# Attention and gated MLP on one core: one planner for all pairs of heads, and score products of 128 rows

## The chip, the core and the metric

The kernel runs on one core of one Trainium2 chip. TensorE (PE) does the matrix products; its weight loads (PEld) run beside them. VectorE (DVE) and ScalarE (ACT) do the element-wise work, GpSimd (POOL) a few constants, and SyncE (SP) issues the transfers. Each engine works through its own list of instructions in order and waits at semaphores for the others. The metric is the device time of one execution in microseconds (us); lower is better.

## The reference

```python
# q, k, v: (4 batches, 8 heads, 768 tokens, 64), n_sink = 4, window = 128
scores = (1 / np.sqrt(D)) * np.matmul(q, k.transpose(0, 1, 3, 2))
keep = is_sink | in_window               # first 4 keys, or 0 <= i - j < 128
scores = np.where(keep, scores, -1e9)
a = exp(scores - max);  a = a / (sum(a) + 1e-09)
attn = np.matmul(a, v)                   # then laid out as x: 3072 tokens x 512
h = x @ w_in                             # 512 x 2048
g = h * np.clip(h + 3.0, 0.0, 6.0) / 6.0
out = g @ w_out                          # 2048 x 512
```

All of it is float32.

## The kernel before, in words

**Tiles.** A *unit* is 256 tokens of one batch: 12 units. The first tokens of the four batches come first (units 0 to 3), then the other eight. A *pair* is two heads of one unit: 48 pairs, four to a unit. A pair goes through these steps, named by the letters of the task table: `kq` and `v` load K, Q and V; `C` makes the scores on PE (line 497, tile `sp`); `t` masks and finds the minimum (DVE, L507), `m` merges the two windows (L515), `x` is the exponential (ACT, L524), `c` the reciprocal sums, `n` scales the rows (L538/L540); `D` transposes the probabilities on PE (L562, tile `pt`); for pairs of later units `p` multiplies by a side mask (L572, tile `pm`); `o` and `ol` split the result into a high and a low part (L195, L598, tiles `ph` and `pl`); `E` multiplies by V on PE (L640, tile `av`); `a`, `b`, `y`, `xh`, `xl` add up and split the result into the MLP's input `xh` and `xl`. A unit's MLP has 8 chunks; in each, `F` is 2 halves of 12 products (L698, tile `hps`), then `r`, `s`, `h`, `g` on ACT and DVE (L707 to L716), and `G` is 2 halves of 6 products (L730, tile `o`).

**Precision.** Values are split into a high and a low float32r part, and a product is the sum of three partial products. Pairs 0 to 11 use plain float32 products for attention instead. The scores of pairs 12 to 47 are three partial products for each of two heads and two tiles of queries. K and Q of the two heads lie on partitions 0 to 63 and 64 to 127, so each of these products uses 64 rows of the array:

```python
terms = [(d["qt"][:, i, ts], d["kt"][:, j, ks]) for i, j in ((0, 0), (1, 0), (0, 1))]
for j, (l, r) in enumerate(terms):
    for g in range(2):
        gs = slice(D * g, D * (g + 1))
        nc.tensor.matmul(out=sp[g][:, 0:w], lhsT=l[gs], rhs=r[gs], ...)
```

**Order.** Two mechanisms set the order. For pairs 0 to 13, the 32 parts of the weights and the MLP of units 0 and 1, `first_tasks` lists tasks with a cost, what they come after, a due number and what room they take (PSUM banks, buffers). `in_order` goes through time: whenever an engine is free it takes the ready task with the lowest due number that has room. Until planned time 30 (`QUIET`) an idle PE gets a filler product (tile `idle`, L245). A weight part is loaded (`w`), rebuilt from 64-bit words on ACT and DVE (`wa` to `wd`, L333 to L341) and split (`wh`, `wl`, L346). From pair 14 on `STAGES` writes the order by hand: eight stages for a pair, in which three pairs overlap (prepare, score, multiply by V), and `drain(1)` puts one half of an MLP chunk behind each stage. So each pair brings two chunks of MLP.

The names `wih`/`wil` and `woh`/`wol` are the high and low parts of the 8 chunks of both weights, `kt` and `qt` the split K and Q, `kr` and `qr` what was loaded.

Of the kernel before, what the change touches and what calls it, by code (L numbers as in the profile page):

```python
# [28 lines left out]
PAIRS = 14  # L29
NF32 = 12  # L30
PART_DUE = (5.4, 14.1, 33.8, 61.6, 65.3, 70.3, 72.6, 72.7, 75.9, 78, 80, 86.7, 102.5, 103.4, 105.5, 115, 115.2, 116.3,
            118.3, 119.3, 120.2, 122.7, 123.4, 124.1, 124.2, 124.4, 141.9, 161.5, 187.6, 205, 220.3, 236.5)
LEAD = {"kq": 39.1, "v": 38.1, "w": 38.8}
QUIET = 30.0
ROOM = {"kq": 2, "V": 2, "vr": 1, "split": 1, "bank": 7, "pl": 2, "Pt": 1, "ph": 2, "st": 3, "vs": 1, "wt": 3, "gf": 2,
        "gh": 2, "x0": 2, "x1": 2, "x2": 2, "x3": 2}


def first_tasks():
# [7 lines left out]
    for s in range(PAIRS):  # L47
        d = 10 * s
        f32 = s < NF32
        add(f"kq{s}", "SP", 0.95, [], d - LEAD["kq"], ("kq",))  # L50
        add(f"v{s}", "SP", 0.47, [], d - LEAD["v"], ("V",) if f32 else ("V", "vr"))
        start = [f"kq{s}"]
        if not f32:
            add(f"kh{s}", "ACT", 0.31, [f"kq{s}"], d - 1, ("split",))
            add(f"kl{s}", "DVE", 0.335, [f"kh{s}"], d - 1)
            add(f"qh{s}", "ACT", 0.31, [f"kq{s}", f"kh{s}"], d - 1)
            add(f"ql{s}", "DVE", 0.335, [f"qh{s}"], d - 1, (), ("kq",))
            add(f"vh{s}", "ACT", 0.31, [f"v{s}"], d + 3)
            add(f"vl{s}", "DVE", 0.335, [f"vh{s}"], d + 3, (), ("vr",))
            start = [f"kl{s}", f"ql{s}"]  # L60
        if s == PAIRS - 1:
            continue
        hold = ("pl", "pl") if f32 and s % 2 else ("Pt",)
        add(f"C{s}", "PE", 0.8 if f32 else 1.0, start, d, ("bank",) * 4 + hold, ("kq",) if f32 else ("split",), 0.35)
        for t in range(2):
            for h in range(2):
                add(f"t{s}.{t}{h}", "DVE", 0.345 if t else 0.21, [f"C{s}", "mask"], d + 0.1, (), ("bank",))
                add(f"x{s}.{t}{h}", "ACT", 0.49 if t else 0.385, [f"t{s}.{t}{h}"], d + 0.2)
        add(f"c{s}", "DVE", 0.41, [f"x{s}.{t}{h}" for t in range(2) for h in range(2)], d + 0.3, lag=0.1)
        for h in range(2):  # L70
            for t in range(2):
                add(f"n{s}.{t}{h}", "*", (0.41, 0.27) if t else (0.3, 0.2), [f"c{s}"], d + 0.4 + 0.01 * h)
            gives = hold[h:h + 1] if len(hold) == 2 else hold if h else ()
            add(f"D{s}.{h}", "PE", 0.4, [f"n{s}.0{h}", f"n{s}.1{h}"] + [f"D{s}.0"] * h, d + 0.5,
                ("bank", "ph") if f32 else ("bank", "ph", "pl"), gives)
            if f32:
                add(f"o{s}.{h}", "ACT", 0.37, [f"D{s}.{h}"], d + 0.6, (), ("bank",))
            else:
                add(f"o{s}.{h}", "ACT", 0.41, [f"D{s}.{h}"], d + 0.6)
                add(f"ol{s}.{h}", "DVE", 0.45, [f"o{s}.{h}"], d + 0.6, (), ("bank",))  # L80
        if f32:
            add(f"E{s}.0", "PE", 0.68, [f"o{s}.0", f"v{s}"], d + 0.7, ("bank", f"x{s % 4}"), ("ph",))
            add(f"E{s}.1", "PE", 0.68, [f"o{s}.1", f"E{s}.0"], d + 0.7, (), ("ph", "V"))
            add(f"xh{s}", "ACT", 0.27, [f"E{s}.1"], d + 0.8)
            add(f"xl{s}", "DVE", 0.334, [f"xh{s}"], d + 0.9, (), ("bank",))
    for k in range(32):
# [9 lines left out]
    for n in range(2):  # L96
        xs = [f"xl{4 * n + p}" for p in range(4)]
        for i in range(8):
            d = 1000 + 100 * n + 5 * i
            before = [f"F{n}.{i - 1}.1"] if i else []  # L100
            add(f"F{n}.{i}.0", "PE", 1.42, xs + before + [f"wl{4 * i}", f"wl{4 * i + 1}"], d, ("bank",))
            add(f"F{n}.{i}.1", "PE", 1.42, [f"F{n}.{i}.0"], d + 0.1, (), ("x0", "x1", "x2", "x3") if i == 7 else (), 0.25)
            add(f"r{n}.{i}", "ACT", 0.57, [f"F{n}.{i}.1"], -50, ("gf",))
# [3 lines left out]
            before = [f"G{n}.{i - 1}.1"] if i else []  # L107
            add(f"G{n}.{i}.0", "PE", 1.4, before + [f"g{n}.{i}", f"wl{4 * i + 2}", f"wl{4 * i + 3}"], d + 1.5,
                () if i else ("bank", "bank"))
            add(f"G{n}.{i}.1", "PE", 1.4, [f"G{n}.{i}.0"], d + 1.6, (), ("gh",))  # L110
        for t in range(2):
            add(f"O{n}.{t}", "ACT", 0.54, [f"G{n}.7.{t}"], -50, ("st",), ("bank",))
# [4 lines left out]
def in_order(tasks):  # L117
# [15 lines left out]
    while marks:  # L133
# [9 lines left out]
        while moved:  # L143
            moved = False
            for k, e in enumerate(engines):
# [25 lines left out]
                if gives:  # L171
                    heapq.heappush(freed, (end, count, gives))
                    heapq.heappush(marks, end)
# [31 lines left out]
def attn_ffn_kernel(ctx: ExitStack, tc: tile.TileContext, qx, kx, vx, vfx, vsx, n_sink, window, w_in, w_out, out):  # L205
# [190 lines left out]
    XHF = "A"  # L396
# [4 lines left out]
    def A_kq(s):  # L401
# [5 lines left out]
        st_[s].update(kr=kr, qr=qr)  # L407

# [15 lines left out]
    def A_split(s, part=None):  # L424
        if "vr" not in st_[s]:
            return
        hi, lo, src = st_[s]["vr"]
        if part != 1:
            copy_r(nc, nc.scalar, hi, src)
        if part != 0:  # L430
            nc.vector.tensor_tensor(out=lo, in0=src, in1=hi.bitcast(F32), op=ALU.subtract)
            del st_[s]["vr"]

    def B_k(s, part=None):
        if plain(s):
            return
        w = ncol(pus[s][1])
        d = st_[s]  # L440
# [32 lines left out]
    def C_score(s):  # L473
# [3 lines left out]
        d["nb"], d["sm"], d["rc"] = (work.tile([P, 4], F32, name=x, bufs=3) for x in ("nb", "sm", "rc"))  # L477
        if not plain(s):
            d["P"] = work.tile([P, 2, 2, WP], F32, name="Pt", bufs=1)
        elif s % 2:  # L480
            d["P0"], d["P1"] = (work.tile([P, 3 * P], F32, tag="pl", name="Ph") for h in range(2))
        else:
            both = work.tile([P, 2, 3 * P], F32, tag="Pt", name="Ph", bufs=1)
            d["P0"], d["P1"] = both[:, 0, :], both[:, 1, :]
        d["sp"] = []
        for t, (k0c, w, m) in enumerate(spans(u)):
# [569 lines left out]
```

## Time and profile before

| | us |
|---|---|
| median of 3 runs | 707.57 (707.29 to 707.86) |
| the profiled execution's own time | 706.91 |
| its span, first to last instruction | 705.1 |
| PE busy | 695.7 (99%) |
| PE weight loads busy | 618.5 (88%) |
| DVE busy | 514.7 (73%) |
| ACT busy | 455.8 (65%) |

The span is what the instructions cover; the execution's own time has some 1.8 us around it. Matmuls are pipelined: one lasts longer than the distance to the next, so busy PE time says little, and the distance from start to start is what counts. Granted TensorE clock was 0.998 of full speed over the span.

### The profile page before, as it was taken

To read this page: it belongs to the slowest core of one execution; us is meant where nothing else is said; L and a number is where in the kernel's file an instruction comes from. 1 tells how busy PE (TensorE), PEld (TensorE's weight loads), DVE (VectorE), ACT (ScalarE), POOL (GpSimd) and SP (SyncE) were. 2 spreads that over 40 slices of the span, in tenths; PEclk is the share of its full clock that TensorE was granted. 3 is DMA by queue.
4 is the path that set the end of the run, shared out by engine and by line. 5 is a ranking of instruction groups with operands and counts; after the bars stand their busy time and mean duration, and the time that the engine had idled before them with its cause. 6 is when DMAs were issued, how large, how long until landed. Compare 5 with 4: busy or idle time off the path is not lost.

```text
span 705.1 us, 13207 instructions
## 1 busy us (share of the span) xinstructions
PE 695.7 (99%) x4908; PEld 618.5 (88%) x4908; DVE 514.7 (73%) x1359; ACT 455.8 (65%) x1203; POOL 4.5 (1%) x18
## 2 busy tenths in 40 slices
PE   8999999999999999999999999999999999999996
PEld 7888988889898889898989898989898989899995
DVE  5999997455678778777877788778777877785221
ACT  5999886665576666657666667567656765764222
POOL 2000000000000000000000000000000000000000
PEclk9999999999999999999999999999999999999999
DMA  7665562220111101211111112111110111100000
GB/s 253 196 215 190 192 202 70 76 68 27 43 61 61 32 31 61 63 41 62 32 59 64 31 43 76 46 32 61 56 48 31 61 54 39 61 13 2 31 1 34
DMA packets 29608, 49.69 MB, mean 70 GB/s; under 512 B 3552, under 2 KB 20448, under 8 KB 29536
## 3 DMA queue, kind: packets, MB, share of 16 engines
q1 hardware_dynamic: 29248, 48.77, 21.4%
q8 instruction: 40, 0.66, 0.4%
q14 instruction: 32, 0.26, 0.1%
q10 hardware_dynamic: 288, 0.00, 0.0%
HBM read 42.47 MB, written 6.29 MB: 69 GB/s over the span
## 4 chain that ended last, share of the span: by engine, by line
PE 82%; ACT 6%; DVE 6%; DMA 4%; issue 1%; ACTq 0%; DVEq 0%; SPq 0%
PE o L730 34%; PE hps L698 33%; PE av L640 6%; PE sp L497 5%; PE pt L562 3%; DMA st<-in_w_in_dram 2%; ACT Ph L524 2%; DMA st<-in_w_out_dram 1%; DVE st L338 1%; DVE wt L341 1%; ACT wt L333 1%; ACT st L335 1%; ACT Ph L538 1%; PE pt L644 1%; DMA raw<-in_window_dram 1%
## 5 line engine op out<-in xcount | busy, mean ns | idle before, releaser
L698 PE MATMUL hps<-xh,wih 128*128 128x256 f32 x768 | 223.0, 290 | 0.0
L698 PE MATMUL hps<-xh,wil 128*128 128x256 f32 x768 | 216.5, 282 | 0.0
L698 PE MATMUL hps<-xl,wih 128*128 128x256 f32 x768 | 215.8, 281 | 0.0
L730 PE MATMUL o<-woh,gh 128*128 128x512 f32 x384 | 155.7, 406 | 0.1
L730 PE MATMUL o<-woh,g 128*128 128x512 f32 x384 | 151.8, 395 | 0.7 <-DVE g L716 0.7
L730 PE MATMUL o<-wol,gh 128*128 128x512 f32 x384 | 151.0, 393 | 0.0
L698 PEld LDWEIGHTS hps<-xh,wih 128*128 128x128 f32 x768 | 144.8, 189 | 2.1 <-issue 0.7
L698 PEld LDWEIGHTS hps<-xl,wih 128*128 128x128 f32 x768 | 144.9, 189 | 1.2
L698 PEld LDWEIGHTS hps<-xh,wil 128*128 128x128 f32 x768 | 144.6, 188 | 0.0
L710 DVE SCALAR_TENSOR_TENSOR gf<-gf,hps 128x512 f32<-128x512 f32 x96 | 65.6, 684 | 52.5 <-ACT gf L707 52.2
L707 ACT ACTIVATE gf<-hps,three 128x512 f32<-128x512 f32 x96 | 65.4, 681 | 55.2 <-PE hps L698 54.9
L716 DVE TENSOR_TENSOR g<-gf,gh 128x512 fp32r<-128x512 f32 x96 | 66.3, 691 | 35.6 <-ACT gh L195 35.4
L730 PEld LDWEIGHTS o<-woh,g 128*128 128x128 f32 x384 | 72.1, 188 | 18.1 <-DVE g L716 1.6
L730 PEld LDWEIGHTS o<-woh,gh 128*128 128x128 f32 x384 | 72.3, 188 | 16.5 <-issue 2.8
L730 PEld LDWEIGHTS o<-wol,gh 128*128 128x128 f32 x384 | 72.5, 189 | 11.0
L195 ACT ACTIVATE ph<-pm 128x512 fp32r<-128x512 f32 x64 | 40.4, 632 | 64.0 <-DVE pm L572 64.0
L598 DVE TENSOR_TENSOR pl<-pm,ph 128x512 fp32r<-128x512 f32 x64 | 44.3, 692 | 44.7 <-ACT ph L195 44.7
L195 ACT ACTIVATE gh<-gf 128x512 fp32r<-128x512 f32 x91 | 57.0, 626 | 26.6 <-DVE gf L710 25.8
L524 ACT ACTIVATE Pt<-Pt,nb 128x144 f32<-128x144 f32 (+2 forms) x144 | 58.7, 409 | 2.3 <-DVE Pt L515 1.2
L507 DVE CUSTOM_DVE_ANT_0 Pt<-sp,m_t 128x272 f32<-128x272 f32 x128 | 48.5, 435 | 0.0
L667 ACT COPY tmp<-av 64x256 f32<-64x256 f32 x72 | 26.5, 368 | 33.0 <-PE av L640 32.5
L538 ACT ACTIVATE Pt<-Pt,rc 128x144 f32<-128x144 f32 (+2 forms) x142 | 47.6, 408 | 0.0
(102 smaller groups left out, 960.0 us busy)
## 6 DMA issues: line engine op xcount, KB each, us to landing
st<-in_w_in_dram SPq DMA_DIRECT2D x16, 512.0 KB, 4.6
st<-in_w_out_dram SPq DMA_DIRECT2D x16, 512.0 KB, 4.4
kr<-in_kx_dram SPq DMA_DIRECT2D x32, 200.0 KB, 2.6
qr<-in_qx_dram SPq DMA_DIRECT2D x48, 128.0 KB, 2.8
out_dram<-ost SPq DMA_DIRECT2D x24, 256.0 KB, 2.1
vr<-in_vx_dram SPq DMA_DIRECT2D x32, 192.0 KB, 2.4
VF<-in_vfx_dram SPq DMA_DIRECT2D x12, 256.0 KB, 3.2
kr<-in_kx_dram SPq DMA_DIRECT2D x16, 128.0 KB, 3.3
```

Of the source, the lines that this page charges most:

```text
L195: nc.scalar.mul(out=out, in_=src, mul=scale)
L497: nc.tensor.matmul(out=sp[g][:, 0:w], lhsT=l[gs], rhs=r[gs], start=(j == 0), stop=(j == len(terms) - 1))
L507: nc.vector.tensor_tensor_reduce(out=cell(s, g, t, 0, w), in0=sp[g][:, 0:w], in1=m[:, 0:w], scale=-SCALE, scalar=3.0e38, op0=ALU.add, op1= ...
L524: nc.scalar.activation(out=blk, in_=blk, func=AF.Exp, scale=-1.0, bias=d["nb"][:, i:i + 1], accum_out=d["sm"][:, i:i + 1])
L538: nc.scalar.mul(out=blk, in_=blk, mul=c)
L598: nc.vector.tensor_tensor(out=pl[:, 0:w], in0=pt[:, 0:w], in1=ph[:, 0:w].bitcast(F32), op=ALU.subtract)
L640: nc.tensor.matmul(out=o, lhsT=l, rhs=r, start=(j == 0 and (h == 0 or not plain(s))), stop=(j == len(seq) - 1 and (h == 1 or not plain(s))))
L698: nc.tensor.matmul(out=hp[:, half, :], lhsT=l, rhs=r, start=(j == 0), stop=(j == n - 1))
L707: nc.scalar.activation(out=gf, in_=hp, func=AF.Relu, bias=three, scale=1.0)
L710: nc.vector.scalar_tensor_tensor(out=gf, in0=gf, scalar=6.0, in1=hp, op0=ALU.min, op1=ALU.mult)
L716: nc.vector.tensor_tensor(out=g, in0=gf, in1=gh.bitcast(F32), op=ALU.subtract)
L730: nc.tensor.matmul(out=acc, lhsT=l[:, f, ts_], rhs=r[i][:, f, :], start=(i == 0 and f == 0 and j == 0), stop=(i == NFP - 1 and f == 1 and ...
```

## The change

`first_tasks` becomes `all_tasks`: all 48 pairs and 12 units are in one table, and `STAGES`, `stage`, `drain` and the queues are gone. The planner also gains `MARGIN` (0.6 is added before a PE task that depends on another engine) and `GIVEN` (0.25 before room counts as free). Due numbers of the weight parts and the loads are others.

For pairs 12 to 47, K is loaded twice (once for each half of the partitions), so that each head's 64 rows lie on both halves; Q as well. K is split so that the upper half holds the high part and the lower half the low part; Q has the high part on both halves, and its low part on both. A product of 128 rows is then high and low at once, and four such products make what six of 64 rows made. The scores are cut into two tasks, `C.0` and `C.1`, one for each tile of queries.

```diff
-PAIRS = 14
+PAIRS = 48
+UNITS = PAIRS // 4
-LEAD = {"kq": 39.1, "v": 38.1, "w": 38.8}
+LEAD = {"kq": 45.2, "v": 30.4, "w": 24.5}
+LATE = 1007.1
+GLAG = 19.6
+MARGIN = 0.6
+GIVEN = 0.25
...
+            add(f"ka{s}", "SP", 0.95, [], d - AHEAD["load"], ("kd",))
+            add(f"qa{s}", "SP", 0.95, [], d - AHEAD["load"] + 0.1, ("qd",))
+            add(f"kh{s}", "*", (0.86, 0.5) if far else (0.54, 0.336), [f"ka{s}"], d - AHEAD["kt"], ("kt",))
+            add(f"kl{s}", "DVE", 0.905 if far else 0.61, [f"kh{s}"], d - AHEAD["kt"] + 0.1, (), ("kd",))
...
+            add(f"C{s}.0", "PE", 0.5 if far else 0.44, [f"kl{s}", f"ql{s}"], d, ("bank", "bank", "Pt"), (), 0.35)
+            add(f"C{s}.1", "PE", 0.5 if far else 0.475, [f"C{s}.0"], d + 0.05, ("bank", "bank"), ("kt", "qt"), 0.35)
...
-                    heapq.heappush(freed, (end, count, gives))
+                    heapq.heappush(freed, (end + GIVEN, count, gives))
...
-                    at[nxt] = max(at[nxt], end + lag)
+                    apart = 0.0 if tasks[nxt][0] == e else lag + MARGIN * (tasks[nxt][0] == "PE")
+                    at[nxt] = max(at[nxt], end + apart)
...
+    def A_far(s, which):
+        b, u, p = pus[s]
+        w, src = (ncol(u), kx) if which == "k" else (UT, qx)
+        t = work.tile([P, 2, 400 if which == "k" else UT], F32, name=f"{which}d", bufs=1)
+        for half in ROWS:
+            nc.sync.dma_start(out=t[half, :, 0:w], in_=src[b, u, p, :, 0:w].rearrange("(h d) c -> d h c", h=2))
...
-            copy_r(nc, nc.scalar, d["kt"][:, 0, 0:w], d["kr"][:, 0:w])
+            copy_r(nc, e, d["kt"][:, :, 0:w], d["kr"][:, :, 0:w])
+        else:
+            low = d["kt"][ROWS[1], :, 0:w]
+            nc.vector.tensor_tensor(out=low, in0=d["kr"][ROWS[1], :, 0:w], in1=low.bitcast(F32), op=ALU.subtract)
...
-                terms = [(d["qt"][:, i, ts], d["kt"][:, j, ks]) for i, j in ((0, 0), (1, 0), (0, 1))]
+                for i in range(2):
+                    nc.tensor.matmul(out=sp[g][:, 0:w], lhsT=d["qt"][:, i, g, ts], rhs=d["kt"][:, g, ks],
+                                     start=(i == 0), stop=(i == 1))
...
-    for s in range(FROM, NS + 2):
-        for steps in STAGES:
-            stage(s, steps)
-            drain(1)
-            tick()
+    for name, e, _ in in_order(all_tasks()):
+        do(name, e)
```

What this moves shows at three places. First PE in the steady part, around the scores of one pair (`sp`); before:

```order
L730 MATMUL o_8030<-woh_128,g 128x512
L497 MATMUL sp<-kt,qt 128x272 x12
L730 MATMUL o_8047<-woh_128,gh 128x512
L730 MATMUL o_8047<-wol_136,gh 128x512
L730 MATMUL o_8047<-woh_128,g 128x512
L730 MATMUL o_8047<-woh_128,gh 128x512
L730 MATMUL o_8047<-wol_136,gh 128x512
L730 MATMUL o_8047<-woh_128,g 128x512
L640 MATMUL av<-ph,VS 128x256
```

and after, from the end of `E.0` to the start of `E.1`:

```order
L675 MATMUL av<-ph,VS 128x128
L538 MATMUL sp<-kt,qt 128x272 x4
L761 MATMUL o_7974<-woh_128,gh 128x512
L761 MATMUL o_7974<-wol_136,gh 128x512
L761 MATMUL o_7974<-woh_128,g 128x512
L761 MATMUL o_7974<-woh_128,gh 128x512
L761 MATMUL o_7974<-wol_136,gh 128x512
L761 MATMUL o_7974<-woh_128,g 128x512
L675 MATMUL av<-ph,VS 128x256
```

Twelve products in one piece have become four here, behind `E.0`, and four more behind `E.1`. Before, the scores and one half of `G` stood on each side between the transposes and the first product with V; now `E.0` follows the transposes `D.0` with two halves of `F` and `D.1` between them in most periods.

Second DVE in the same part, from the scaling of the sink scores (`ssc`) over the two masks (`pm`) and low parts (`pl`) on; before:

```order
L716 TENSOR_TENSOR g<-gf,gh 128x512
L201 CAST ssc<-Pt 128x2x32
L190 TENSOR_TENSOR ssc<-Pt,ssc 128x2x32
L572 TENSOR_TENSOR pm<-pt,side 128x512
L598 TENSOR_TENSOR pl<-pm,ph 128x512
L572 TENSOR_TENSOR pm<-pt,side 128x512
L598 TENSOR_TENSOR pl<-pm,ph 128x512
L710 SCALAR_TENSOR_TENSOR gf<-gf,hps 128x512
```

and after:

```order
L581 TENSOR_SCALAR Pt<-Pt,rc 128x144 x2
L746 TENSOR_TENSOR g<-gf,gh 128x512
L592 TENSOR_TENSOR ssc<-Pt,ssc 128x2x32
L613 TENSOR_TENSOR pm<-pt,side 128x512
L635 TENSOR_TENSOR pl<-pm,ph 128x512
L613 TENSOR_TENSOR pm<-pt,side 128x512
L635 TENSOR_TENSOR pl<-pm,ph 128x512
L740 SCALAR_TENSOR_TENSOR gf<-gf,hps 128x512
```

The masks and low parts alternate as before; DVE has taken two of the four scalings and given one copy (`ssc`) to ACT.

Third PE early, where the last chunk of `w_in` (`wih_116`) is first used; before:

```order
L698 MATMUL hps<-xh_804,wil_123 128x256
L730 MATMUL o_1128<-woh_129,gh 128x512
L730 MATMUL o_1128<-wol_137,gh 128x512
L730 MATMUL o_1128<-woh_129,g 128x512
L730 MATMUL o_1128<-woh_129,gh 128x512
L730 MATMUL o_1128<-wol_137,gh 128x512
L730 MATMUL o_1128<-woh_129,g 128x512
L698 MATMUL hps<-xh_262,wih_116 128x256
```

and after:

```order
L728 MATMUL hps<-xh_833,wil_122 128x256
L761 MATMUL o_805<-woh_131,gh 128x512
L761 MATMUL o_805<-wol_139,gh 128x512
L761 MATMUL o_805<-woh_131,g 128x512
L761 MATMUL o_805<-woh_131,gh 128x512
L761 MATMUL o_805<-wol_139,gh 128x512
L761 MATMUL o_805<-woh_131,g 128x512
```

Counted from the start of the program up to the first product with `wih_116`, PE has the same 11 scores, 9 transposes, 8 products with V and 22 halves of `G` in both; halves of `F` are 27 before and 25 after, and fillers 46 and 57.

## Rows read from the trace of the kernel before

**Rows 1.** Window table: stretch, us, busy (x) of PE PEld DVE ACT POOL, PEclk, DMA.
```profile
9.00:31.00 22.00, 20.87 (x155) 17.13 (x154) 20.05 (x87) 21.91 (x73) 0.00 (x0) 1.00 0.76 249
31.00:116.00 85.00, 84.82 (x562) 74.92 (x563) 81.00 (x188) 75.88 (x171) 0.00 (x0) 1.00 0.58 188
153.00:632.00 479.00, 479.00 (x3482) 427.67 (x3481) 369.94 (x971) 314.45 (x864) 0.00 (x0) 1.00 0.15 48
```

**Rows 2.** Chain that ended last, one steady period: start us, us, what.
```profile
222.55 2.84 PE hps L698 x24
225.39 2.79 PE o L730 x12
228.18 0.22 PE pt L562 x2
228.40 1.42 PE hps L698 x12
...
230.17 1.43 PE hps L698 x12
...
235.50 1.00 PE av L640 x12
236.51 0.17 PE pt L644
236.68 2.85 PE hps L698 x24
```

**Rows 3.** Timeline of PE around one pair's scores: start us, us, instruction.
```profile
416.40 0.39 PE L730 MATMUL o<-woh,g 128*128 128x512 f32 x1
416.72 1.02 PE L497 MATMUL sp<-kt,qt 64*128 64x272 f32 x12
417.67 0.50 PE L730 MATMUL o<-woh,gh 128*128 128x512 f32 x1
418.00 0.40 PE L730 MATMUL o<-wol,gh 128*128 128x512 f32 x1
```

**Rows 4.** Timeline of PE, DVE and ACT from one pair's first transposes to their low part.
```profile
411.84 0.38 PE L562 MATMUL pt<-ident_r,Pt 128*128 128x128 f32 x2
...
412.75 0.68 DVE L572 TENSOR_TENSOR pm<-pt,side 128x512 f32<-128x512 f32 x1
413.47 0.64 ACT L195 ACTIVATE ph<-pm 128x512 fp32r<-128x512 f32 x1 [0.60 <-DVE pm L572]
414.14 0.69 DVE L598 TENSOR_TENSOR pl<-pm,ph 128x512 fp32r<-128x512 f32 x1 [0.70 <-ACT ph L195]
```

**Rows 5.** Filler products alone, in the first two stretches of the window table.
```profile
0.00:9.00 9.00, 6.61 (x37) 6.32 (x38) 1.00 0.62 191
9.00:31.00 22.00, 7.58 (x57) 6.69 (x55) 1.00 0.76 249
```

**Rows 6.** Timeline where the last weights arrive: DVE, then PE.
```profile
115.13 0.69 DVE L346 TENSOR_TENSOR wil<-wt,wih 128x512 fp32r<-128x512 f32 x1
...
115.49 0.28 PE L698 MATMUL hps<-xh,wih 128*128 128x256 f32 x1
117.16 0.40 PE L730 MATMUL o<-wol,gh 128*128 128x512 f32 x1
118.28 0.50 PE L730 MATMUL o<-woh,g 128*128 128x512 f32 x1 [0.72 <-DVE g L716]
```

**Rows 7.** Waits of DVE between 9 and 116 us: total, times, longest.
```profile
DVE sm L529 <- ACT Ph L524: 2.1, 4, 1.0
DVE gf L710 <- ACT gf L707: 1.6, 2, 1.2
```

**Rows 8.** Groups by line and form: busy us, mean ns, idle before.
```profile
L447 DVE TENSOR_TENSOR kt<-kr,kt 128x400 fp32r<-128x400 f32 x32 | 18.2, 568 | 0.0
L459 DVE TENSOR_TENSOR qt<-qr,qt 128x256 fp32r<-128x256 f32 x36 | 15.0, 418 | 0.0
L538 ACT ACTIVATE Pt<-Pt,rc 128x144 f32<-128x144 f32 x128 | 42.4, 404 | 0.0
```

More of the change, by code (lines that the diff above doesn't have):

```diff
@@ L47, in first_tasks @@
     for s in range(PAIRS):
[L48 to L60, printed above, removed]
@@ L65, in first_tasks @@
         for t in range(2):
             for h in range(2):
-                add(f"t{s}.{t}{h}", "DVE", 0.345 if t else 0.21, [f"C{s}", "mask"], d + 0.1, (), ("bank",))
-                add(f"x{s}.{t}{h}", "ACT", 0.49 if t else 0.385, [f"t{s}.{t}{h}"], d + 0.2)
-        add(f"c{s}", "DVE", 0.41, [f"x{s}.{t}{h}" for t in range(2) for h in range(2)], d + 0.3, lag=0.1)
+                cost = 0.36 if far else 0.345 if t else 0.21
+                add(f"t{s}.{t}{h}", "DVE", cost, [scores[t], "mask"], d + 0.1, (), ("bank",))
@@ new lines, in all_tasks @@
+                before = [f"m{s}"] if far else [f"t{s}.{t}{h}"]
+                add(f"x{s}.{t}{h}", "ACT", 0.4 if far else 0.49 if t else 0.385, before, d + 0.2)
+        if far:
+            add(f"m{s}", "DVE", 0.61, [f"t{c}" for c in cells], d + 0.15)
+        add(f"c{s}", "DVE", 0.41, [f"x{c}" for c in cells], d + 0.3, lag=0.1)
+        for c in cells:
+            cost = (0.31, 0.21) if far else (0.41, 0.27) if c[-2] == "1" else (0.3, 0.2)
+            add(f"n{c}", "*", cost, [f"c{s}"], d + 0.4 + 0.01 * int(c[-1]))
@@ L70, in first_tasks @@
+        if far:
+            add(f"Sh{s}", "*", (0.25, 0.12), [f"n{c}" for c in cells], d + 0.45, ("ssc",))
+            add(f"Sd{s}", "*", (0.25, 0.115), [f"Sh{s}"], d + 0.46)
+            add(f"Sl{s}", "DVE", 0.145, [f"Sh{s}"], d + 0.46)
         for h in range(2):
-            for t in range(2):
-                add(f"n{s}.{t}{h}", "*", (0.41, 0.27) if t else (0.3, 0.2), [f"c{s}"], d + 0.4 + 0.01 * h)
             gives = hold[h:h + 1] if len(hold) == 2 else hold if h else ()
-            add(f"D{s}.{h}", "PE", 0.4, [f"n{s}.0{h}", f"n{s}.1{h}"] + [f"D{s}.0"] * h, d + 0.5,
-                ("bank", "ph") if f32 else ("bank", "ph", "pl"), gives)
@@ L76, in first_tasks @@
-            if f32:
[L77 to L80, printed above, removed]
+            before = [f"n{c}" for c in cells if c[-1] == str(h)] + [f"D{s}.0"] * h
+            if far and h:
+                before += [f"Sd{s}", f"Sl{s}"]
+                gives += ("ssc",)
+            takes = ("bank", "ph") if f32 else ("bank", "wt") if far else ("bank",)
@@ new lines, in all_tasks @@
+            add(f"D{s}.{h}", "PE", 0.33 if not far else 0.36 if h else 0.22, before, d + 0.5, takes, gives, 0.3)
+            last = ("bank",) if not far or not h else ()
+            if f32:
+                add(f"o{s}.{h}", "ACT", 0.37, [f"D{s}.{h}"], d + 0.6, (), last)
+                continue
+            if far:
+                add(f"p{s}.{h}", "DVE", 0.605, [f"D{s}.{h}"], d + 0.55, (), last)
+                last = ("wt",)
+            add(f"o{s}.{h}", "*" if far else "ACT", (0.54, 0.336) if far else 0.41, [f"{'p' if far else 'D'}{s}.{h}"], d + 0.6, ("ph",))
@@ L86, in first_tasks @@
+        add(f"xh{s}", "*", (0.31, 0.2), [f"y{s}" if far else f"b{s}.1"], d + 0.85)
+        add(f"xl{s}", "DVE", 0.334, [f"xh{s}"], d + 0.9, (), ("tmp",))
     for k in range(32):
@@ L471, in cell, with C_score @@
         return st_[s]["P"][:, h, t, c0:c1]
-    def C_score(s):
+    def C_score(s, tiles=(0, 1)):
         b, u, p = pus[s]
         d = st_[s]
[L477 to L486, printed above, removed]
+        if 0 in tiles:
+            d["nb"], d["sm"], d["rc"] = (work.tile([P, 4], F32, name=x, bufs=3) for x in ("nb", "sm", "rc"))
+            d["sp"] = []
+            if not plain(s):
+                d["P"] = work.tile([P, 2, 2, WP], F32, name="Pt", bufs=1)
+            elif s % 2:
+                d["P0"], d["P1"] = (work.tile([P, 3 * P], F32, tag="pl", name="Ph") for h in range(2))
+            else:
+                both = work.tile([P, 2, 3 * P], F32, tag="Pt", name="Ph", bufs=1)
+                d["P0"], d["P1"] = both[:, 0, :], both[:, 1, :]
+        for t in tiles:
+            k0c, w, m = spans(u)[t]
             ts, ks = slice(t * P, (t + 1) * P), slice(k0c, k0c + w)
@@ L718, in ffn1 @@
             state["post", i] = (relu, gate, high, low)
-            post(1, relu, gate)
-            post(2, high, low)
+            if not planned:
+                for step in state["post", i]:
+                    step()
     def ffn2(i, tt, psum, state, tag):
```

304 lines of the change are left out of this document (119 added, 185 removed).

## The prediction

> **What bounds the kernel now.** I read the window table first, because a busy share over the whole span hides stages. From 153 to 632 us PE is busy 479.00 of 479.00 us, while DVE has 369.94 (77%) and ACT 314.45 (66%) [rows 1]. Busy matmuls overlap, so this alone does not prove that PE sets the pace; the chain of waits does. In it a whole period of one pair is PE from end to end, with no wait for another engine: it starts at 222.55 and the next at 236.68, so a period is 14.13 us [rows 2]. The granted clock is 1.00 there, the 2.4 GHz level [rows 1]. A period has 48 products for `F`, at 2.84 per 24, and 24 for `G`, at 2.79 per 12 [rows 2]: 5.68 + 5.58 = 11.26 us. The other 2.87 us are the pair's attention. In the steady part only PE's own work counts.
>
> Before 116 us it is otherwise. From 9 to 31 us PE has fillers for 7.58 of its 20.87 busy us [rows 1, 5], and ACT is busy for 21.91 of 22.00, DVE for 20.05. From 31 to 116 us DVE has 81.00 of 85.00 [rows 1]. The last part of the last `w_in` chunk starts its low part on DVE at 115.13 and ends it at 115.82; PE starts the first product with that chunk at 115.49 [rows 6]. So PE and DVE arrive there together: weight preparation on DVE paces this stage, and PE's order was fitted to it.
>
> **The change part by part.** I sum against the profiled execution's 706.91 us; the median of the runs shown is 707.57, so 0.66 is added at the end.
>
> *Scores of pairs 16 to 47.* From the start of the last `G` product ahead of them (416.40) to the second one behind (418.00) are 1.60 us [rows 3]. Two `G` products take 2 x 2.79/12 = 0.465, so the scores cost PE 1.135 us. The new ones are 8 products of 128 rows and 272 columns. No row has that shape in a stream; 256 columns go at 2.84/24 = 0.118 and 512 at 2.79/12 = 0.2325 [rows 2], and the line between them gives 0.125 for 272. So 8 x 0.125 = 1.00 and a gain of 0.135 us each, 32 x 0.135 = 4.3 us. Bounds: at 0.118 each it is 32 x 0.19 = 6.1 gained; the other end is a rival below. I take 4.3, since both shapes lie on either side.
>
> Where do the old 1.135 us come from? Twelve products in concurrent twos would be six slots, 6 x 0.125 = 0.75. The other 0.385 stands at the edges: the last `G` ahead is 0.32 from the scores instead of 0.23, and the first behind is 0.33 from the next [rows 3]. Switching between 64 and 128 rows eats what concurrency gives, and the change removes the switch.
>
> Here a rule of the Trainium skill speaks against the change: its page "TensorE: Matmul & The Clock Gate", in "Why this matters for your kernels", says that products with few rows should lie on distinct row groups, since they then run concurrently and a small product alone takes as long as a full one. By that rule 8 full slots replace 6, and each pair would lose 0.25 us. The Trainium skill's "TensorEngine Tiling (Array Packing)", under "Key Properties", sets against it that a change of tiling mode drains the array. The trace bears out both: twelve products lie within 1.02 us [rows 3], fewer than twelve times 0.118, and 0.385 us are lost at the edges.
>
> *Scores of pairs 12 to 15.* The same count of products with 128 and 256 columns; the gain is between 0 and 4 x 0.2 = 0.8 us by the same reckoning. I take 0.5.
>
> *More pieces.* Scores and the products with V are now cut in two, with `G` or nothing between. The V products end with one of 256 columns that takes 0.17 where such a one needs 0.118 [rows 2], 0.05 for leaving them. If each of 32 additional pieces paid that, 1.6 us; since one such step already sits between the two halves of a pair's V products (12 take 1.00 in the chain [rows 2] where 8 of 128 columns, at 0.061 by the same line, and 4 of 256 need 0.96), it is moved rather than added. I take 0; bounds 0 to 1.6.
>
> *DVE, ACT and the loads.* The low part of K is now 800 elements on 64 partitions instead of 400 on 128 (568 ns), Q's 512 instead of 256 (418 ns) [rows 8]. By 512-element work at 0.69 [rows 4] Q's grows by 0.27; K's is at most doubled, +0.57. Two of four scalings go from ACT (404 ns each [rows 8]) to DVE, at most +0.81. So DVE has up to 1.65 us more in a period, 12.6 of 14.13 or 89% instead of 77%; of the smaller copies some move to DVE and some (`ssc`, `xh`) to ACT. PE's own work covers this, and it costs nothing unless the order is tight (rival 1). K and Q loads double, but DMA is at 0.15 there [rows 1].
>
> *The window between D.0 and E.0.* This wait is new. Before, 7.3 us lay between them (228.18 to 235.50 [rows 2]); now `E.0` follows two halves of `F` and `D.1`. From the start of `D.0` that is 0.22 + 1.42 + 0.35 + 1.43 = 3.42 us [rows 2]. The chain it needs was 411.84 to 414.83, or 2.99 us, of which 0.9 went by before DVE began with the mask [rows 4]. So 0.4 us are left at least. If `E.0` waits, the scores, `G` and `E.1` queue behind it on PE, and nothing fills that. I take 0.3 us in all for pairs off the rhythm; bounds 0 and the rival.
>
> *The start.* At the first product with the last `w_in` chunk PE has done the same work before and after, but two halves of `F` less: 2 x 1.42 = 2.84 us that it must still do later. If DVE delivers at 115.8 as before, that is lost. Two things come back: the stall behind this chunk, 118.28 - 117.16 = 1.12 where 0.23 is due [rows 6], 0.9 us, since `G` is further there; and part of DVE's own waits, 2.1 + 1.6 us [rows 7], as two `F` halves fewer mean one chunk less of `s` and `g` ahead of the weights (2 x 0.6), against K and Q of pair 12 in the wide form. Of 3.7 I take half, 1.9. So 2.84 - 0.9 - 1.9 = 0. Bounds: +2.8 with nothing given back, -1.8 with all of it. The 11 additional fillers sit in time in which PE has nothing else, and cost nothing of their own. K and Q of pair 12 are now issued before those of the third pair, four issues of SP; the third pair's scores ran long after its load, so this is covered.
>
> *The tail* stays: `F` and `G` alone, then the output.
>
> Sum: -4.3 - 0.5 + 0 + 0.3 + 0 = -4.5. 706.91 - 4.5 = 702.4 for a profiled execution, and 703.1 for the median.
>
> **Rivals.**
>
> 1. *E.0 waits for its low part* (slower). Place: each period, at the first V product. DVE has `ssc`, two masks, two low parts and MLP steps in one list; if one operation of 0.61 more stands ahead of a mask or low part, the chain is 2.99 + 0.61 = 3.60, and with 0.05 to PE 3.65 against 3.42. That is 0.23 x 32 = 7.4 us: 703.1 + 7.4 = 710.5. It decides from 0.14 us a pair, where it eats the 4.5. For it: the chain had 7.3 us before, and DVE gets fuller. Against it: the order of masks and low parts is unchanged, and 0.9 us of the chain were other DVE work.
>
> 2. *Concurrency is lost, the switch is not saved.* The edges could belong to starting a new accumulation on fresh banks and not to 64 rows. Then the new scores are 1.00 + 0.385 = 1.385, 0.25 more than before: 32 x 0.25 = 8 us instead of -4.3, and the median 703.1 + 12.3 = 715.4. Against it: `F` and `G` also start on fresh banks, and in the chain 24 of them take 2.84 with no edge [rows 2]. This is what the Trainium skill's rule on row groups in "TensorE: Matmul & The Clock Gate" would give.
>
> 3. *The start eats it* (no change). DVE delivers as late as before, PE falls 2.84 behind, and a stall like the one at 117 us comes at another place (0.9): +3.7, 706.8. For it: DVE was busy 81 of 85 us, so there is little to win. Against: the waits of 3.7 us.
>
> 4. *The start gives more*: DVE's waits go altogether, -1.8, and the scores go at 0.118, -1.8: 699.5.
>
> **How the numbers follow.** The forecast 0.56, between 701 and 705; rival 1 0.13, rival 2 0.05, rival 3 0.16, rival 4 0.10. The range 699.5 to 707.5 leaves out rivals 1 and 2 and the edge of 3. What a measurement can tell from no change is 0.2%, 1.4 us: faster is below 706.15. The forecast, rival 4 and nearly half of rival 3 lie there: 0.73. The other half of 3 and a weak form of 1: 0.11 the same. The rest, 0.16, slower.
>
> **What would show it.** Right: the steady period is shorter by about 0.13 us where it has two chunks, the starts of the score products are 0.125 apart, and the last `G` product ahead of them is 0.23 from them. Wrong: 0.3 or more at those edges (rival 2); waits of PE's products `av` for DVE `pl`, on many pairs (rival 1); the first product with the last `w_in` chunk at 116 us or later, with PE waiting for `wil` or `wih` ahead of it (rival 3). What would make the prediction wrong outright is a wait in the steady part that repeats, since every 0.1 us of it costs 3.2.

## The result and the profile after

The kernel after takes 701.82 us (median of 4 runs, 700.9 to 701.83) against 707.68 for the kernel before beside it: ratio 0.9915, 95% interval 0.9897 to 0.9932. The forecast was 703.1. Its profiled execution took 701.83 us; the sum had 702.4.

From the page after, busy time, share of the span and instructions of each engine:

```profile
PE 691.4 (99%) x4786; PEld 632.6 (90%) x4786; DVE 559.3 (80%) x1396; ACT 458.6 (66%) x1166; POOL 4.5 (1%) x18
```

The window table, columns as in [rows 1]:

```profile
9.00:31.00 22.00, 21.78 (x170) 19.09 (x171) 20.91 (x74) 21.51 (x68) 0.00 (x0) 1.00 0.93 289
31.00:116.00 85.00, 84.09 (x558) 74.58 (x557) 82.57 (x198) 74.36 (x170) 0.52 (x1) 1.00 0.56 181
...
153.00:632.00 479.00, 479.00 (x3379) 443.28 (x3378) 415.98 (x1029) 323.23 (x846) 0.00 (x0) 1.00 0.25 71
```

From 153 to 632 us PE is as full as in [rows 1]; DVE went from 369.94 to 415.98 us (87%), less than the 89% that the prediction allowed. Now one period in the chain, to set beside [rows 2]:

```profile
403.10 2.87 PE hps L728 x24
405.97 2.75 PE o L761 x12
408.72 0.22 PE pt L603 x2
408.94 1.44 PE hps L728 x12
...
412.16 0.47 PE av L675 x6
412.63 0.57 PE sp L538 x4
413.20 1.39 PE o L761 x6
414.59 0.47 PE av L675 x6
415.06 0.17 PE pt L679
415.22 0.50 PE sp L538 x4
415.72 1.37 PE o L761 x6
417.09 2.87 PE hps L728 x24
```

It is PE from end to end, 13.99 us (403.10 to 417.09) where it was 14.13. The reader should see two things: `av` follows one half of `F` without a wait for `pl`, and the scores are two pieces, of 0.57 and 0.50 us, with no 0.33 behind either. The edges of one piece on PE's timeline, to set beside [rows 3]:

```profile
414.89 0.33 PE L679 MATMUL pt<-pz,vs 128*128 128x256 f32 x1
415.06 0.66 PE L538 MATMUL sp<-kt,qt 128*128 128x272 f32 x4
415.56 0.39 PE L761 MATMUL o<-woh,gh 128*128 128x512 f32 x1
415.79 0.40 PE L761 MATMUL o<-wol,gh 128*128 128x512 f32 x1
```

Four products in 0.50 us, and the first `G` product 0.23 ahead of the next; before it was 0.33. Over the whole trace the score products start 0.126 apart (median). Twenty-four middle pairs with the same work in both kernels (1152 products of `F`, 576 of `G`) took 339.36 us before and 335.94 after: -0.1425 a pair, forecast -0.135. What this is made of stands under "Why the prediction was right".

The window from `D.0` to `E.0`, to set beside [rows 4]:

```profile
408.56 0.38 PE L603 MATMUL pt<-ident_r,Pt 128*128 128x128 f32 x2
...
409.69 0.68 DVE L613 TENSOR_TENSOR pm<-pt,side 128x512 f32<-128x512 f32 x1
...
410.41 0.63 ACT L249 ACTIVATE ph<-pm 128x512 fp32r<-128x512 f32 x1 [1.14 <-DVE pm L613]
...
411.07 0.69 DVE L635 TENSOR_TENSOR pl<-pm,ph 128x512 fp32r<-128x512 f32 x1 [0.70 <-ACT ph L249]
...
412.00 0.34 PE L675 MATMUL av<-ph,VS 128*128 128x256 f32 x2
```

3.44 us are there (forecast 3.42). The low part ends at 411.76 and `av` starts at 412.00, so 0.24 us are left: tight, but no wait.

The start, to set beside [rows 6]: the low part of the last `w_in` chunk, and its first product.

```profile
110.98 0.69 DVE L397 TENSOR_TENSOR wil<-wt,wih 128x512 fp32r<-128x512 f32 x1
```

```profile
113.62 0.28 PE L728 MATMUL hps<-xh,wih 128*128 128x256 f32 x1
```

DVE is there 4.1 us earlier, 2 us ahead of PE, and the stall of [rows 6] is gone; DVE waits for 1.5 us between 9 and 116 where the list of [rows 7] and its smaller entries came to 4.8. In exchange there is one new stall, and more fillers than in [rows 5] (10.88 us in the second stretch):

```profile
66.23 0.48 PE L535 MATMUL sp<-kr,qr 64*128 64x256 f32 x1 [0.71 <-DVE nb L548]
```

### The profile page after: what moved, and what is told of

It reads as the page before. It is cut to its first block, busy times and chain, and to the rows that moved or that the text cites. A ratio compares the mean times of both kernels' runs of the same rounds, so it can differ in the third digit from the quotient of the medians.

```text
span 699.9 us, 13133 instructions
## 1 busy us (share of the span) xinstructions
PE 691.4 (99%) x4786; PEld 632.6 (90%) x4786; DVE 559.3 (80%) x1396; ACT 458.6 (66%) x1166; POOL 4.5 (1%) x18
## 4 chain that ended last, share of the span: by engine, by line
PE 90%; DVE 5%; DMA 2%; ACT 2%; issue 1%; ACTq 0%; DVEq 0%
PE hps L728 37%; PE o L761 37%; PE av L675 6%; PE sp L538 5%; PE pt L603 3%; DVE Ph L548 1%; PE pt L679 1%; DMA st<-in_w_out_dram 1%; DVE wt L392 1%; DVE st L389 1%; DMA raw<-in_window_dram 1%; DMA st<-in_w_in_dram 1%; PE pt L601 1%; ACT Ph L565 1%; DVE Ph L581 0%
## 5 line engine op out<-in xcount | busy, mean ns | idle before, releaser
L761 PE MATMUL o<-woh,gh 128*128 128x512 f32 x384 | 153.2, 399 | 0.0
L728 PEld LDWEIGHTS hps<-xh,wih 128*128 128x128 f32 x768 | 146.9, 191 | 2.8 <-DVE nb L548 0.3
L728 PEld LDWEIGHTS hps<-xl,wih 128*128 128x128 f32 x768 | 147.2, 192 | 2.1
L728 PEld LDWEIGHTS hps<-xh,wil 128*128 128x128 f32 x768 | 147.0, 191 | 0.0
L249 ACT ACTIVATE ph<-pm 128x512 fp32r<-128x512 f32 x61 | 38.6, 632 | 61.8 <-DVE pm L613 61.8
L249 ACT ACTIVATE gh<-gf 128x512 fp32r<-128x512 f32 x66 | 41.6, 630 | 26.0 <-DVE gf L740 26.0
L548 DVE CUSTOM_DVE_ANT_0 Pt<-sp,m_t 128x272 f32<-128x272 f32 x128 | 51.3, 432 | 0.0
L538 PE MATMUL sp<-kt,qt 128*128 128x272 f32 (+2 forms) x288 | 46.9, 292 | 0.0
L613 DVE TENSOR_TENSOR pm<-pt,side 128x512 f32<-128x512 f32 x64 | 43.8, 684 | 0.6
```

The costliest lines, as they stand in the source:

```text
L249: nc.scalar.mul(out=out, in_=src, mul=scale)
L538: nc.tensor.matmul(out=sp[g][:, 0:w], lhsT=d["qt"][:, i, g, ts], rhs=d["kt"][:, g, ks], start=(i == 0), stop=(i == 1))
L548: nc.vector.tensor_tensor_reduce(out=cell(s, g, t, 0, w), in0=sp[g][:, 0:w], in1=m[:, 0:w], scale=-SCALE, scalar=3.0e38, op0=ALU.add, op1= ...
L613: nc.vector.tensor_tensor(out=pm, in0=pt.unsqueeze(2).to_broadcast([P, 2, 2, P]), in1=side.unsqueeze(1).to_broadcast([P, 2, 2, P]), op=ALU ...
L728: nc.tensor.matmul(out=hp[:, half, :], lhsT=l, rhs=r, start=(j == 0), stop=(j == n - 1))
L761: nc.tensor.matmul(out=acc, lhsT=l[:, f, ts_], rhs=r[i][:, f, :], start=(i == 0 and f == 0 and j == 0), stop=(i == NFP - 1 and f == 1 and ...
```

## The experiments

**1. Undo the form of the scores, keep the order.**

```diff
-                for i in range(2):
-                    nc.tensor.matmul(out=sp[g][:, 0:w], lhsT=d["qt"][:, i, g, ts], rhs=d["kt"][:, g, ks], ...)
+                terms = [(d["qt"][:, i, ts], d["kt"][:, j, ks]) for i, j in ((0, 0), (1, 0), (0, 1))]
+                for j, (l, r) in enumerate(terms):
+                    for g in range(2):
+                        nc.tensor.matmul(out=sp[g][:, 0:w], lhsT=l[gs], rhs=r[gs], ...)
```

> The kernel after with its order of work kept, but with the score products of the kernel before: K and Q are loaded once and split on 128 partitions, and each score piece of pairs 12 to 47 is 64-row products again, six for one tile of queries where four of 128 rows would make two (C.0 and C.1 each 6 instead of 4, twelve where both stand together). Theory (a switch between 64 and 128 rows costs some 0.385 us each time, and the change saves it): the trace of after has 42 single pieces and 11 double ones among the late pairs. A single piece then takes 3 x 0.125 + 0.385 = 0.76 us instead of 4 x 0.125 = 0.50, a double one 0.135 more: 42 x 0.26 + 11 x 0.135 = 12.4, and about 0.5 for pairs 12 to 15: 701.8 + 12.9 = 714.7 us (712 to 717), with edges of 0.3 us and more around each score piece. Rival (the gain is the planner's order, and the form of the scores is neutral): 701.8 +- 1 us. Rival 2 of the prediction (the edge belongs to fresh accumulations, concurrency is what counts): two products of 64 rows run in one slot, 3 slots for 4, so 64 pieces are 0.125 faster each: 694 us.

Measured: 705.31 us (704.32 to 705.98): 3.5 us more than the kernel after, where 12.9 were expected. Yet the pieces are as dear as expected. One of them on PE's timeline:

```profile
418.26 0.33 PE L681 MATMUL pt<-pz,vs 128*128 128x256 f32 x1
418.52 0.64 PE L541 MATMUL sp<-kt,qt 64*128 64x272 f32 x6
419.10 0.50 PE L763 MATMUL o<-woh,gh 128*128 128x512 f32 x1
419.43 0.40 PE L763 MATMUL o<-wol,gh 128*128 128x512 f32 x1
```

From the `z` transpose to the second `G` product are 1.17 us, against 0.90 in the kernel after: +0.27 a piece, expected +0.26. So something else became faster. In the chain of this run 24 products of `F` take 2.74 us, where the kernel after needs 2.87, and `F` starts every 0.1134 us even behind 645 us, where no attention runs. This sent me to the places of the tiles (experiments 5 to 8).

**2. The form of the scores alone, in the old order.** PE's order is that of before, with eight products where twelve stood.

```diff
+    t = work.tile([P, 2, 400 if which == "k" else UT], F32, name=f"{which}d", bufs=1)
+    for half in ROWS:
+        nc.sync.dma_start(out=t[half, :, 0:w], ...)
...
-    for j, (l, r) in enumerate(terms):   # 64 rows, three terms, two heads
+    for i in range(2):                   # 128 rows, two terms, two heads
```

> The kernel before with its order of PE's work kept word for word, and only the scores of pairs 12 to 47 changed: K and Q loaded twice, split in the wide form, eight products of 128 rows in one piece where twelve of 64 rows stood. Theory (the steady gain is the score form's own): 34 pairs of the steady part at 0.14 us = 4.8, pairs 12 and 13 some 0.2 each: 707.6 - 5 = 702.6 us (701.5 to 704.5; the start may cost up to 1.5 since the wide K and Q of the 13th and 14th pair come on top of DVE's weight work), with no repeated wait of PE in the steady part. Rival (the longer DVE operations do not fit the old hand-written order, so the planner is needed): 706 us or more, with PE waiting for kt, qt or pl in most periods.

Measured: 718.57 us (717.49 to 719.69), ratio 1.0152 (1.0138 to 1.0166). The theory failed, but not at the scores; the rival's time holds, with waits at another place than it named. On PE's timeline:

```profile
409.14 0.40 PE L735 MATMUL o<-woh,g 128*128 128x512 f32 x1
409.37 1.17 PE L502 MATMUL sp<-kt,qt 128*128 128x272 f32 x8
410.37 0.39 PE L735 MATMUL o<-woh,gh 128*128 128x512 f32 x1
410.61 0.40 PE L735 MATMUL o<-wol,gh 128*128 128x512 f32 x1
```

From the last `G` product ahead to the second behind are 1.47 us; before it was 1.60 [rows 3], and the forecast was 1.465; the mean over 24 pairs fell by 0.139. The loss is elsewhere: the chain of waits of this run is no longer PE.

```profile
399.87 0.99 DVE kt L455
400.86 0.01 issue
400.87 0.69 DVE qt L465
...
404.60 0.43 DVE xl L689
405.03 0.60 DVE g L721
405.63 0.12 DVE ssc L201
...
406.63 0.64 ACT ph L195
...
414.17 0.99 DVE kt L455
```

DVE with ACT between goes round in 14.30 us (399.87 to 414.17), longer than PE's own work. PE comes to the transposes of the scaled sink scores and they are not there; one of the dearest such places:

```profile
334.63 0.27 PE L565 MATMUL pt<-ident_r,ssc 128*96 128x128 f32 x1 [0.47 <-ACT ssc L195]
```

In 24 pairs the step from `F` to `D` grew from 2.86 to 9.55 us, and the pairs from 339.36 to 345.84. That is 6.5 of the 12.0 us between the two profiled executions; some 4 more arise before these pairs, among them a step of 2.53 us from `F` to `G` at 93 us. DVE is busy only 389 of 479 us there: a share of 81% did not show that its list was the limit.

**3. The new order without its margins.**

```diff
-MARGIN = 0.6
-GIVEN = 0.25
+MARGIN = 0.0
+GIVEN = 0.0
```

> The kernel after with MARGIN and GIVEN at 0 instead of 0.6 and 0.25: the plan then puts a PE task at the moment at which its input is planned to be ready. Theory (E.0 was not late because the plan keeps 0.6 us between the end of its chain and its start; the prediction's window of 3.42 us was too small a reading of it): 704 to 712 us, with PE waits for DVE (pl, nb, kt) or ACT named in many periods. Rival (PE has enough other work anyway, the margin decides nothing): 701 to 703 us, with no more PE waits than the kernel after (2.2 us).

Measured: 720.23 us (719.95 to 720.45), ratio 1.0178 (1.0163 to 1.0194): the theory's side, with a price of 18 us where it said at most 10. The waits are again at the transposes (group of one line, 153 to 632 us; the last part is idle time and its releasers):

```profile
L601 PE MATMUL pt<-ident_r,ssc 128*96 128x128 f32 x60 | 14.0, 290 | 7.0 <-ACT ssc L249 4.3 <-DVE ssc L255 2.6
```

In the kernel after the same group has 0.0 idle. With the same work (1152 products of `F`, 576 of `G`) 24 pairs took 346.71 us here and 335.94 after, 10.8 more; from one transpose to the next they took 20.99 and 8.20. So the loss of the pairs is at `D`, not at `E.0`; some 6 us more are lost ahead of these pairs. `MARGIN` and `GIVEN` were taken out together, and the plan orders some work differently without them, so what each is worth stays open.

**4. Pair 12's preparation out of the start.**

```diff
+    tasks["ka12"][2].append("wl31")
+    tasks["qa12"][2].append("wl31")
```

> The kernel after with the loads of K and Q of pair 12 planned only behind the split of the last weight part, so that pair 12's wide preparation does not stand among DVE's weight work. Theory (DVE's own busy time sets how early the weights are done, so 2 to 3 us of DVE work less in front of the last part bring it forward, and PE has fewer fillers or a shorter stall): 700 to 701.3 us, first product with the last w_in chunk earlier by 1 us or more. Rival (by now PE alone sets the end: it does not wait for weights, so DVE work moved out of the start gives nothing): 701.8 +- 0.4 us, or later if pair 12's scores come late.

Measured: 704.85 us (704.02 to 706.26): 3 us worse, which only the rival's last clause allows. The profiled execution is the slowest of the five. In it the first product with the last `w_in` chunk came at 115.4 us, 1.8 us later than in the kernel after; but this delay arises at 66 to 74 us, where the granted clock fell to the 1.2 GHz level (last section), which accounts for some 1.7 us. Without it the product would stand where it stood: no earlier, as the rival has it. The change's own price shows later, where PE waited twice at products with V that come at once in the kernel after:

```profile
192.66 0.45 PE L677 MATMUL av<-ph,VS 128*128 128x256 f32 x2 [0.52 <-ACT ph L251]
193.59 0.44 PE L677 MATMUL av<-pl,VS 128*64 128x128 f32 x2 [0.48 <-DVE pl L637]
```

**5 to 8. Places of the tiles.** One unused tile in front of `xh` moves `xh`, `xl`, `qt` and two of the four buffers of `g` and of `gh` in SBUF, besides a few tiles that PE does not read; in run 7 a second one, ahead of the weights, moves nearly all tiles. The order of work stays.

```diff
+        if s == 0:
+            pad = work.tile([P, 48], F32, name="pad", bufs=1)   # 16 in runs 6 and 8, 40 for 160 bytes
         xh = work.tile([P, UT], F32R, tag=f"xh{p}", name=f"xh{p}")
...
+    padw = const.tile([P, 16], F32, name="padw")                # run 7 only
     WIH = [const.tile([P, NP, 256], F32R, name=f"wih{i}") for i in range(NFP)]
```

> The kernel after with one unused tile of 192 bytes a partition laid in front of the first xh; nothing else is changed, the order is the same. In the run with the old score form on the new order the products of F started 0.1134 us apart, even in the tail where no other work is, while they start 0.1200 apart in the kernel after and 0.1187 apart before; in the built programs xh begins at a byte address that is 192, 0 and 128 beyond a multiple of 256 in the three. This puts it at 192. Theory (the place of the moving tile xh sets the pace of F, and this hid 9 us of what the old score form costs): F at 0.1134, 2304 products x 0.0040 (the difference of the means, edges included) = 9 us less: 692.7 us (691 to 695). Rival (the pace belongs to the form of the scores, to the weight of the other engines' traffic or to the program as a whole): 701.8 +- 0.7 us, F at 0.120.

> The kernel before with one unused tile of 64 bytes a partition in front of the first xh, which brings xh from 128 to 192 beyond a multiple of 256 bytes. Theory (place of xh sets the pace): F from 0.1187 to 0.1134 us, 2304 x 0.0045 = 10 us less: 697.5 us (696 to 700), and against it the kernel after at the same place is 5 us faster, as at the old places. Rival (the pace belongs to something else): 707.6 +- 0.7 us.

> The kernel after with 64 unused bytes in front of the weights (wih from 0 to 64 beyond a multiple of 256, woh too) and 192 in front of xh, so that xh stays at 0 beyond a multiple of 256 and only its distance from the weights is that of the old-scores run. If the place of xh itself counts: F stays at 0.120 us and the time at 701.8 +- 1 us, except what G gains or loses by woh, its moving tile, at 64. If the distance between xh and wih counts: F at 0.1134 and about 693 us.

> The kernel after with an unused tile of 64 bytes a partition in front of the first xh: 64 beyond a multiple of 256. If it counts only whether the place is a multiple of 128: as with 192, F at 0.1134 us and about 693 us. If 192 is a place of its own: F between 0.114 and 0.120, 693 to 702 us.

A further place, 160 bytes, was run with experiments 9 and 10:

> The kernel after with an unused tile of 160 bytes a partition in front of the first xh: a place that is no multiple of 64. So far F starts every 0.1200, 0.1178, 0.1187 and 0.1134 us with xh 0, 64, 128 and 192 beyond a multiple of 256 (wih at 0), and 0.1134 with xh at 0 and wih at 64, so that the distance between the two tiles counts. If 160 lies between its neighbours: F 0.113 to 0.119, and 698 to 702 us. If there are still better places: under 0.113. If multiples of 64 are better in themselves: over 0.120, more than 702 us.

The distances below are from the addresses in the built programs. The median is taken over stretches of twelve products.

| kernel | `xh` less `wih`, bytes modulo 256 | `F`, median us from start to start | us |
|---|---|---|---|
| after | 0 | 0.1200 | 701.82 |
| run 8 (after, 64) | 64 | 0.1178 | 701.75 |
| before | 128 | 0.1187 | 707.68 |
| after, 160 | 160 | 0.1186 | 702.46 |
| run 5 (after, 192) | 192 | 0.1134 | 697.68 |
| run 6 (before, 64 more) | 192 | 0.1134 | 699.81 |
| run 7 (weights 64, `xh` 0) | 192 | 0.1134 | 698.69 |
| run 1 (old scores) | 192 | 0.1134 | 705.31 |

For the pace of `F` the place theory holds in each; its times were missed in runs 5 and 7 (693 expected). Run 5 has ratio 0.9858 (0.9837 to 0.9878) to before, run 6 0.989 (0.987 to 0.991). Run 7 fits the distance between the two tiles: neither place alone has its old value, the distance is that of run 5, and so is the pace. Run 8 had `F` 4.3 us faster in sum and `G` 3.5 slower (267.4 to 271.0), so `G` depends on places too. Inside bursts of the 24 pairs it starts every 0.229 to 0.230 us in the kernels whose distance above is 0 or 192, and every 0.232 to 0.233 where it is 64, 128 or 160; why is not shown. But run 5 gave 4.1 us where 9 were expected. Its `F` did gain 9.5 us in sum (280.5 to 271.0). In the 24 middle pairs `F` inside its bursts gained 5.2 us, and the transposes and the steps to and from them lost 4.4 in sum (`D` to `D` 2.2, `F` to `D` 1.0, `D` to `F` 0.7, `G` to `D` 0.4). Run 5 and the kernel after around one `D.1`:

```profile
407.18 0.22 DVE L592 TENSOR_TENSOR ssc<-Pt,ssc 128x64 fp32r<-128x64 f32 x1
...
407.55 0.27 PE L601 MATMUL pt<-ident_r,ssc 128*96 128x128 f32 x1
```

```profile
409.56 0.22 DVE L592 TENSOR_TENSOR ssc<-Pt,ssc 128x64 fp32r<-128x64 f32 x1
...
410.21 0.23 PE L601 MATMUL pt<-ident_r,ssc 128*96 128x128 f32 x1
```

In run 5 the transpose starts 0.15 us behind the end of `ssc`, in the kernel after 0.43: 0.28 us of slack are used up, and PE is there before its input. Over the 24 pairs the steps into transposes of `ssc` lost 1.2 of the 4.4 us and those into transposes of `Pt` 2.4. Both tiles come from DVE and ACT, but no run shows which of the two sets the time: DVE is busy for 417.78 us of 153 to 632, hardly more than in the kernel after.

**9, 10 and 11. A plan for the faster F.** Run 5 with 1.36 for a half of `F` in the plan; the same with a larger margin; and 1.36 only from the third unit on.

```diff
-            add(f"F{n}.{i}.0", "PE", 1.42, ...)
+            add(f"F{n}.{i}.0", "PE", 1.36, ...)                   # runs 9 and 10; F{n}.{i}.1 likewise
+            add(f"F{n}.{i}.0", "PE", (1.42, 1.36)[n >= 2], ...)   # run 11
...
-MARGIN = 0.6
+MARGIN = 0.9                                                      # run 10 only
```

> The kernel after with xh at 192 beyond a multiple of 256 bytes, and the planner told what F then costs: 1.36 us for a half of twelve products instead of 1.42. With xh moved alone, F gained 5.2 us in 24 pairs and the transposes D and their edges lost 4.6, since PE now comes 0.06 earlier for each half than the plan reckons and stands before the transposes of probabilities that are not there yet. Theory (the plan's costs must follow the pace, its 0.6 of margin then covers again): D and its edges back from 18.0 to about 14 us in 24 pairs, 692 to 695.5 us. Rival (DVE and ACT, now nearly full, set the period at 13.96 us whatever the plan): 696.5 to 699 us.

> The kernel of the run with F at 1.36 in the plan, with MARGIN at 0.9 instead of 0.6. Theory (the waits at the transposes are what the margin is for; without any the run was 18 us slower): no waits left in the steady part, 692 to 695 us, the same or up to 1.5 us below the run with 0.6. Rival (room, not margin, is short: a later E or D holds Pt, banks and buffers longer): 697 us or more.

> The kernel after with xh at 192 beyond a multiple of 256 bytes, and F at 1.36 us in the plan only for the units from the third on; the start keeps the plan of 1.42. With 1.36 everywhere the 24 middle pairs took 334.05 us instead of 335.11, but the new plan of the start had a wait of 1.78 us at 50 us and products at the 1.2 GHz level behind it. Theory (the two are independent: the steady part gains 0.9 to 1.2 us from the right cost, the start loses if it is planned anew): 696.5 us (695.5 to 697.2), no wait over 1.2 us before 116 us. Rival (DVE, 89% busy, sets the period, and what the start does not lose is waited for later): 697.7 +- 0.4 us as with xh moved alone.

Measured: 698.2 (697.52 to 698.98), 700.74 (700.51 to 701.4) and 697.26 us (696.0 to 697.99). Runs 9 and 10 end in the range of their rivals, run 11 between its two. All three bring the 24 pairs from 335.11 to about 334.1 us, and their profiled executions lose it at the start: from one product to the next run 9 has 1.78 us at 50 us, run 10 2.59, and in run 11, which keeps the start's plan, the clock fell at 68 us (last section). In runs 9 and 11 the steps into transposes of `ssc` are down to 3.6 us (5.12 in run 5, 3.92 in the kernel after), so the right cost of `F` does cure that wait; 12.7 us into those of `Pt` (14.52 and 12.09) remain. The interval of run 11 to before (0.9846 to 0.9879) holds run 5's ratio of 0.9858, so whether it gains is open. Runs 5 and 11 are the fastest kernels, some 4 us below the kernel after.

## Why the prediction was right, point by point

- **The scores of pairs 16 to 47** (-0.135 each) were the right term: where PE's order stays they fell by 0.139 (run 2, mean of 24 pairs). That the whole pair comes to -0.1425 in the kernel after is a sum of other parts: the scores with their edges fell from 1.138 to 1.052 us (-0.086), since a piece behind `E` takes 0.56 and not 0.50, and the products with V in two pieces from 1.005 to 0.954 (-0.051). Rival 2 is dead: 0.12 to 0.13 from the last score product to `G`, and no 0.33 behind it. Run 5 against run 1, the same order and the same place of `xh` with both forms, is worth 7.6 us in sum, since in this order the scores are cut into more pieces and 64 rows pay the switch at each.
- **More pieces, 0**: right in sum for 128 rows. The step at the edge went from the products with V to the piece of scores behind them, as the numbers above show.
- **DVE costs nothing, covered by PE**: right for this kernel, but the reason was too simple. The cover is not PE's work alone but the new order and its margin: in the old order the same form, with the same DVE work, ends 11 us slower than before (run 2), and the new order without its margins 18 slower than with them (run 3). The prediction gave rival 1 0.13 and put the danger at `E.0`; it is real, in neighbouring kernels, and lies at `D`: in runs 2 and 3 PE waits there for `ssc`, which in run 2's chain comes behind the long `kt` and `qt`. At `E.0` 0.24 us are left.
- **The start, 0**: somewhat better. Up to the end of pair 16, PE's time without `F` and `G` (0.1190 and 0.2325 us each) fell from 69.71 to 68.02 us, -1.7, where pairs 12 to 15 (-0.5) and one scoring of the steady term (-0.1) were expected. DVE's waits fell by 3.3 us where half of 3.7 was taken. A stall did come elsewhere (1.09 us from start to start at 65 us), as rival 3 had it, without eating the rest. Run 4 shows no gain from moving pair 12 out of the start.
- **What the sum did not know, and luck**: both kernels stand at slow places of `xh`, 128 and 0, and these differ little, by chance: inside bursts of the 24 pairs `F` went from 0.1186 to 0.1198 us, about 1.4 us more in sum, and `G` from 0.2320 to 0.2289, about 1.8 less. No term had either, and they nearly cancel. Had the new tiles moved `xh` to 192, as run 1's did, the same change would have come out 4 us lower. At 192 for both, order and form together bring 2.1 us (699.81 to 697.68) and not 5.9, because there PE of the kernel after comes to its transposes too early (run 5) and that of the kernel before hardly does: its 24 pairs fell from 339.36 to 335.56 us with the place, those of the kernel after from 335.94 to 335.11. At this place the new order with the old form is 5.5 us slower than the old order (705.31 against 699.81): neither half of the change helped alone in these runs.

## What to carry to other kernels

Where a wider form of data takes switches off the engine that sets the pace, look for its price in the order of the engine that prepares it: a busy share of 81% did not show it, and a chain of 14.3 against 14.1 us decided. Before a run is read as the price of an edit, look whether streams that the edit does not touch kept their pace; a tile of another size moves those behind it.

## What was not expected of the hardware

- The same product of 128x128 by 256 columns starts every 0.1134 to 0.1200 us, by the place of the moving tile against the weights in SBUF (table above): its 2304 products took 9.5 us less in the kernel after, whose time fell by 4.1, and 7.5 less in the kernel before, whose time fell by 7.9.
- Twelve products of 64 rows in one piece lose some 0.1 us on each side to the products of 128 rows around them; so do six (run 1: 0.26 instead of 0.17 ahead, 0.33 instead of 0.23 behind).
- After the same 1.09 us stall at 65 us the clock stayed at 1.00 in the kernel after and in run 5, and fell to the 1.2 GHz level in runs 4 and 11. Window table, columns as in [rows 1]; three stretches of run 11, then the second of them for run 5 and for run 4:

```profile
66.00:68.00 2.00, 1.29 (x5) 0.87 (x6) 2.00 (x7) 1.70 (x6) 0.00 (x0) 1.00 0.04 12
68.00:70.00 2.00, 2.00 (x8) 1.61 (x7) 1.97 (x7) 1.83 (x5) 0.00 (x0) 0.51 0.32 83
70.00:74.00 4.00, 4.00 (x30) 4.00 (x30) 3.99 (x14) 2.74 (x10) 0.00 (x0) 0.82 0.49 155
```

```profile
68.00:70.00 2.00, 2.00 (x16) 1.83 (x15) 1.97 (x7) 1.82 (x5) 0.00 (x0) 1.00 0.28 74
```

```profile
68.00:70.00 2.00, 2.00 (x7) 1.63 (x7) 1.97 (x7) 1.83 (x5) 0.00 (x0) 0.50 0.26 68
```

  In run 11 PE had stood for a part of 66 to 68 us (1.29 of 2.00 busy), in run 5 for nearly the same (1.34); `G` products behind it start 0.427 apart in run 11 instead of 0.23. Each of these is one profiled execution; what decides between the two was not tried.
